# A three-stage FFT, routed-expert and dense kernel: the second stage's weights loaded by SyncE in halves, and its first layer's outputs taken in blocks of 128

## The chip, the cores and the metric

The kernel runs on one core of one Trainium2 chip. The metric is the device time of one execution in microseconds (us). Engines are named as in the profile: PE is TensorE (PEld its weight loads), ACT is ScalarE, DVE is VectorE, POOL is GpSimd, SP is SyncE. SP computes nothing here; it only issues DMA transfers. POOL issues the indirect ones (gathers and scatters by a list of row numbers).

## What is computed

```python
X = np.fft.fft(np.fft.fft(x, axis=1), axis=2)           # x: 8 x 3072 x 256
x = X.real.reshape(24576, 256)
logits = x @ w_gate                                     # 8 experts
e_idx = np.argmax(logits, axis=1)
gate_w = softmax(logits)[e_idx]; eom = sigmoid(x @ w_output_gate)
for e in range(8):                                      # each token to one expert
    m = e_idx == e
    out[m] = gate_w[m] * eom[m, e] * (np.maximum(x[m] @ w1[e], 0) @ w2[e])   # 256 -> 1024 -> 256
h = out @ w_in                                          # 256 -> 2048
return (h * sigmoid(1.702 * h)) @ w_out                 # 2048 -> 256
```

## The kernel before

Every factor of a matmul is held as a high and a low part (`h` and `l`, together nearly fp32), and a product is three matmuls: high by low, high by high, low by high. To split a tensor, ACT copies it into the high part (rounding it) and DVE subtracts that from the source to give the low part.

**Stage 1** (`phase1`, to about 309 us) makes the FFT of eight batches in 32 steps (`t` in the loop of L704), writes the result's rows to the DRAM tensor `xs` (SP, L515), and routes: DVE finds each token's expert and its place (`route`, L520), and POOL scatters row numbers and gate factors into per-expert lists in DRAM (`lst`, L612). Once the first four batches are routed, `cut` (L625) decides which tiles of 256 tokens can already be formed: for 40 tiles (`KA`) the expert (`owners`, L145) and the rows of the lists. `plan` (L778) does the same for the rest during stage 2.

**Stage 2** (`phase2`, L953) runs over 100 tiles of 256 tokens (`NALL`), sorted by expert, so that several tiles in a row belong to one expert. For a tile, POOL gathers the token rows from `xs` (L978, `xr`, two DMAs), PE transposes them (L1011, `xt`), ACT and DVE split them (L1014, L1015). A tile then has four turns `j`. In a turn, `hid` (L1034) makes 256 of the 1024 hidden values (24 matmuls, L1040 to L1042), ACT takes the high part with the ReLU (L1045, `hh`), DVE the low part (L1046, `hl`); `outp` (L1049) adds them to the tile's output (24 matmuls, L1059 to L1061) two turns later. After a tile's last `outp`, ACT scales the output by the gate (L1066, `yr`, two instructions) and POOL scatters the rows to the DRAM tensor `y` (L1068).

The weights of a tile's expert are loaded into one raw buffer per layer (`raw1`, `raw2`, 1 MB each) and split into one of two sets of high and low parts (`wps`, by the tile's parity). While tile `i` runs, `loop` (L1088) splits the weights of tile `i + 1` and asks for those of tile `i + 2`: turns 0 and 1 split `raw1` (two splits a turn, L1031 on ACT and L1032 on DVE), turns 2 and 3 split `raw2`. The loads are POOL gathers of one row per partition, issued at the end of turn 1 (`raw1`) and of turn 3 (`raw2`); a gather overwrites what the splits have just read. The row numbers (`widx`) come from `owners`: where a tile has the same expert as the one before it, 4096 is added, which is out of bounds, and the gather moves nothing.

```python
r1 = raw1.rearrange("p a (q c) -> p a c q", c=NFC)          # L1018
c = slice(2 * j, 2 * j + 2)
h, l, r = ws[i][0][:, :, c], ws[i][1][:, :, c], r1[:, :, c]  # first layer, L1028
h, l, r = ws[i][2][:, c], ws[i][3][:, c], raw2[:, c]         # second layer, L1030
```

Hidden block `c` of the first layer holds the outputs `8 q + c`, so a split of `raw1` reads every eighth element; a split of `raw2` reads unbroken runs. Partition `p` of `raw2` holds the rows `8 p` to `8 p + 7` of `w2`.

Between its own work stage 2 carries two other programs, a piece at a time: `conv.run` (L865) turns the dense layer's weights into stage 3's factors (DVE and some ACT, five pieces a tile; its loads `cv_raw`, 256 KB each, and its stores `scr` are SP's), and `rest` (L1151) issues the list scatters that stage 1 left over, `plan`, and the second list gather.

The program order on every engine is written by hand. `phase2` is a generator that `phase1` resumes: at step `NG - 2` (stage 1's buffers on the right side are given up; the raw buffers are made, SP reads tile 0's expert from `one` into a register and loads `raw1` and `raw2`, POOL gathers the lists, `lt`), at step `NG` (the lists are transposed into `xidx` and `scl`, the first token rows are gathered, tile 0's first layer is split), after the last step (tile 0's transposes and first `hid`), and then at every fourth of the remaining routing steps (L763 to L768), where after each step the rank matmuls that are due are issued (`flush`).

**Stage 3** (`phase3`, L1187) reads `y` and computes the dense layers in a seven-product scheme, PE without a break.

Of the kernel before, what the change touches and what calls it, by code (L numbers as in the profile page):

```python
# [18 lines left out]
P = 128  # L19
# [125 lines left out]
def owners(V, cum, ex, tmp, mi, widx, misc):  # L145

    n = mi.shape[1]
    ea = ex[:, 1 : 1 + n]
    for e in range(E):
        V.scalar_tensor_tensor(ea, mi, cum[:, e : e + 1], ea, ALU.is_ge, ALU.add)  # L150
# [4 lines left out]
    yield 0.3  # L155
    V.scalar_tensor_tensor(widx, ea, float(P), tmp, ALU.mult, ALU.add)
    yield 0.2


def phase1(tc, ctx, I, C, xs, lst, spd, kept, idn, then):  # L160
# [23 lines left out]
    ent, pis, keep, seen, widx, li, one = (kept[k] for k in ("ent", "pi", "keep", "seen", "widx", "li", "one"))  # L184
# [101 lines left out]
    el = cp.tile([P, 2, 3, 2, 8], F32R, name="el", tag="el")  # L286
# [338 lines left out]
    def cut():  # L625
# [14 lines left out]
        tmp = cp.tile([P, 96], F32, name="cut1", tag="el")[:, 0:KA]  # L640
        ni, ones, st, lr, ex = t[:, 0:8].bitcast(I32), t[:, 8:16], t[:, 16:24], t[:, 24:25], t[:, 32 : 33 + KA]
# [8 lines left out]
        V.memset(ex, 0.0)  # L650
        V.memset(ex[:, 0:1], -1.0)
        yield 0.3
        yield from tiles(cum, nt, st, ex, tmp, misc[:, 64 : 64 + KA], widx[:, 0:KA], misc)
        V.tensor_copy(one, ex[:, 1:2])
# [4 lines left out]
        yield 0.3  # L659

    def tiles(cum, nt, st, ex, tmp, mi, widx, misc):
        yield from owners(V, cum, ex, tmp, mi, widx, misc)

        V.tensor_scalar(st, nt, -1.0, float(LR), ALU.mult, ALU.add)
        V.scalar_tensor_tensor(st, cum, misc[:, 40:41], st, ALU.is_le, ALU.mult)
        yield 0.3
# [37 lines left out]
    for t in range(NG + 1):  # L704
        b, g = divmod(t, 4)
        if t == NG - 2:
            assert state["sc"] >= 24 * BC
# [33 lines left out]
        if t:  # L741
# [14 lines left out]
            if t == 4 * BC:  # L756
                queues["route"].append((cut(), BC - 1))
        if t < NG:
            if t:
                dims.append((Z, b, g))  # L760
    then.send((turns, scatter))
    n = 0
    while queues["route"]:  # L763
        step("route")
        flush(True)
        n += 1
        if n % 4 == 0 and n <= 12:
            then.send((None, None))  # L768
    for _ in range(max(0, 3 - n // 4)):
        then.send((None, None))  # L770
# [7 lines left out]
def plan(tc, C, kept, tot, pp):  # L778
# [3 lines left out]
    keep, seen, widx, li = (kept[k] for k in ("keep", "seen", "widx", "li"))  # L782
# [22 lines left out]
    ex = pp.tile([P, 1 + NTM - KA], F32, name="ex")  # L805
    V.memset(ex, 0.0)
    V.memset(ex[:, 0:1], -1.0)
    yield
    yield from owners(V, cum, ex, pp.tile([P, NTM - KA], F32, name="tmp"), mi, widx[:, KA:], misc)
# [143 lines left out]
def phase2(tc, ctx, I, xs, y, lst, scr, kept, C, idn, idf):  # L953
# [8 lines left out]
    hp = pool("p2h", 4, side="right")  # L962
    wps = [pool("p2w0", 1, side="right")]
    xp = pool("p2x", 2, side="right")
    rw = pool("p2r", 1, side="right")
    widx, li, one = (kept[k] for k in ("widx", "li", "one"))
    w1v = I["moe_w1"].rearrange("e (p a) f -> (e p) (a f)", a=2)
    w2v = I["moe_w2"].rearrange("e (p a) d -> (e p) (a d)", a=8)
    xidx = rw.tile([P, 2, 2, P], I32, name="xidx")
    scl = rw.tile([P, 2, P], F32, name="scl")  # L970
    lt = rw.tile([P, 2, P, 3], F32, name="lt")
    raw1 = rw.tile([P, 2, F1], F32, name="raw1")
    raw2 = rw.tile([P, 8, D], F32, name="raw2")
# [19 lines left out]
    def gather_w(i, k):  # L993
        if i < st["end"]:
            raw, src = ((raw1, w1v), (raw2, w2v))[k]
# [493 lines left out]
```

## Time and profile before

| | |
|---|---|
| median of 3 runs | 3627.42 us (3624.44 to 3629.73) |
| the profiled execution | 3622.02 us; its span 3620.1 us |
| mean granted PE clock | 0.987 |
| PE busy | 3492.8 us (96%) |
| DVE busy | 2478.4 us (68%) |
| ACT busy | 2557.9 us (71%) |
| POOL busy | 1186.0 us (33%) |
| DMA packets | 217.06 MB, mean 60 GB/s |

Busy times are of the whole span; a busy PE is not PE at its peak, since matmuls overlap. In rows that group instructions, the columns are: line, engine, operation, output <- inputs, shapes, count | busy time in us, mean ns of one | idle time of the engine just before them in us, and what ended most of it. "SPq" and the like stand for an engine's queue, which waits and issues.

### The profile page before, as it was taken

The numbers are of one execution on the slowest core, as the hardware profiler recorded it, in microseconds if no ns is written. First come the engines' busy times: TensorE is split into PE (matmuls) and PEld (weight loads), VectorE is DVE, ScalarE is ACT, GpSimd is POOL, SyncE is SP. The second block draws the span as 40 slices with busy tenths as digits, with TensorE's granted clock in tenths as the row PEclk, the third lists the DMA queues.
The fourth block names the chain that finished last, engine by engine and source line by source line (L and its number), as shares of the span: only waits on it lengthen the run. The fifth ranks groups of instructions, "written<-read, shape, count | busy, mean of one in ns | idle before, by whom it ended". The sixth has DMA issues, their size and how long they took to land.

```text
span 3620.1 us, 54703 instructions
## 1 busy us (share of the span) xinstructions
PE 3492.8 (96%) x20688; PEld 3118.2 (86%) x20688; DVE 2478.4 (68%) x3977; ACT 2557.9 (71%) x4457; POOL 1186.0 (33%) x988
## 2 busy tenths in 40 slices
PE   6998998999999999979999999999999999999999
PEld 5998898999999999978888888888888888888887
DVE  7886888888999899855555555555555555555554
ACT  5676777777888788856666666666666666666665
POOL 2774777866666666620000000000000000000000
PEclk9999999999999999989999999999999999999999
DMA  9763222222222222220000000000000000000000
GB/s 244 197 172 107 71 86 80 68 78 98 78 71 93 81 92 72 67 93 24 24 24 35 24 24 24 24 24 24 28 31 24 24 33 26 24 24 24 24 12 24
DMA packets 112899, 217.06 MB, mean 60 GB/s; under 512 B 42389, under 2 KB 77590, under 8 KB 102392
## 3 DMA queue, kind: packets, MB, share of 16 engines
q1 hardware_dynamic: 51352, 123.29, 11.0%
q0 software_dynamic: 60976, 89.98, 8.0%
q8 instruction: 163, 2.67, 0.3%
q14 instruction: 104, 0.85, 0.1%
q10 hardware_dynamic: 304, 0.26, 0.0%
HBM read 306.73 MB, written 83.86 MB: 108 GB/s over the span
## 4 chain that ended last, share of the span: by engine, by line
PE 70%; DVE 10%; ACT 8%; DMA 6%; issue 4%; POOL 1%; ACTq 0%; POOLq 0%; DVEq 0%; SPq 0%
PE acc L1370 10%; PE acc L1372 10%; PE acc L1371 10%; PE R L1305 5%; PE R L1307 5%; PE R L1306 5%; DMA raw<-in_moe_w,widx 4%; ACT w1h L1031 4%; DVE w1l L1032 3%; PE Q L1307 2%; PE Q L1305 2%; PE Q L1306 2%; PE yp L1061 2%; PE h L1040 2%; PE yp L1060 2%
## 5 line engine op out<-in xcount | busy, mean ns | idle before, releaser
L1227 DVE TENSOR_TENSOR g<-c,g 128x512 fp32r<-128x512 f32 x768 | 540.7, 706 | 136.9 <-ACT g L1212 128.6
L1370 PE MATMUL acc<-g,W 128*128 128x512 f32 x1536 | 605.7, 394 | 0.0
L1372 PE MATMUL acc<-g,W 128*128 128x512 f32 x1536 | 599.0, 390 | 0.0
L1371 PE MATMUL acc<-g,W 128*128 128x512 f32 x1536 | 598.1, 389 | 0.0
L1310 ACT ACTIVATE c<-c 128x512 f32<-128x512 f32 x576 | 364.7, 633 | 301.7 <-DVE c L1233 301.7
L1031 ACT CAST w1h<-raw 128x512 fp32r<-128x512 f32 x400 | 470.8, 1235 | 140.8 <-DMA raw<-in_moe_w,widx 140.8
L1032 DVE TENSOR_TENSOR w1l<-raw,w1h 128x512 fp32r<-128x512 f32 x400 | 460.2, 1185 | 122.7 <-ACT w1h L1031 121.8
L1230 POOL TENSOR_TENSOR xs<-xf,xf 128x512 f32<-128x512 f32 x46 | 69.9, 1519 | 1375.1 <-ACT g L1212 1375.1
L1212 ACT CAST g<-c 128x512 fp32r<-128x512 f32 x768 | 477.1, 621 | 24.4
L1061 PE MATMUL yp<-w2h,hl 128*128 128x256 f32 x1600 | 461.4, 288 | 30.0 <-DVE hl L1046 29.4
L1059 PE MATMUL yp<-w2l,hh 128*128 128x256 f32 x1600 | 455.7, 285 | 20.8 <-ACT hh L1045 20.7
L1040 PE MATMUL h<-xl,w1h 128*128 128x256 f32 x1600 | 462.1, 289 | 3.3 <-DVE xl L1015 3.3
L1042 PE MATMUL h<-xh,w1l 128*128 128x256 f32 x1600 | 455.4, 285 | 0.0
L1041 PE MATMUL h<-xh,w1h 128*128 128x256 f32 x1600 | 455.3, 285 | 0.0
L1060 PE MATMUL yp<-w2h,hh 128*128 128x256 f32 x1600 | 453.8, 284 | 0.0
L1233 DVE TENSOR_TENSOR c<-Q,u 128x512 f32<-128x512 f32 x192 | 132.8, 692 | 390.1 <-PE Q L1307 390.1
L1212 ACT COPY u<-R 128x512 f32<-128x512 f32 x192 | 112.7, 587 | 326.8 <-PE R L1307 326.8
L1061 PEld LDWEIGHTS yp<-w2h,hl 128*128 128x128 f32 x1600 | 306.7, 192 | 41.9 <-DVE hl L1046 41.4
L1372 PEld LDWEIGHTS acc<-g,W 128*128 128x128 f32 x1536 | 288.3, 188 | 61.2
L1371 PEld LDWEIGHTS acc<-g,W 128*128 128x128 f32 x1536 | 288.6, 188 | 57.4
L1370 PEld LDWEIGHTS acc<-g,W 128*128 128x128 f32 x1536 | 288.3, 188 | 56.9
L1059 PEld LDWEIGHTS yp<-w2l,hh 128*128 128x128 f32 x1600 | 306.9, 192 | 23.2 <-ACT hh L1045 23.2
(297 smaller groups left out, 8630.7 us busy)
## 6 DMA issues: line engine op xcount, KB each, us to landing
xs<-row SPq DMA_DIRECT2D x32, 768.0 KB, 5.5
out<-o SPq DMA_DIRECT2D x24, 1024.0 KB, 3.9
R<-in_xl SPq DMA_DIRECT2D x23, 1024.0 KB, 9.2
r<-y SPq DMA_DIRECT2D x23, 1024.0 KB, 4.7
cv_raw<-in_moe_w_in SPq DMA_DIRECT2D x16, 256.0 KB, 2.9
cv_raw<-in_moe_w_out SPq DMA_DIRECT2D x16, 256.0 KB, 3.7
xr<-xs,xidx POOLq DMA_INDIRECT x200
y<-yr,xidx POOLq DMA_INDIRECT x200
```

The source lines that it names most:

```text
L1031: A.copy(h, r)
L1032: V.tensor_tensor(l, r, h.bitcast(F32), ALU.subtract)
L1040: T.matmul(ps[:, a], w1h[:, dh, fc], xl[:, dh], start=(a == 0 and dh == 0), stop=False, skip_group_check=True)
L1042: T.matmul(ps[:, a], w1l[:, dh, fc], xh[:, dh], start=False, stop=(dh == 1), skip_group_check=True)
L1059: T.matmul(ps[:, s], hh[:, a, c], w2l[:, fc], start=(fc == 0 and s == 0), stop=False, skip_group_check=True)
L1060: T.matmul(ps[:, s], hh[:, a, c], w2h[:, fc], start=False, stop=False, skip_group_check=True)
L1061: T.matmul(ps[:, s], hl[:, a, c], w2h[:, fc], start=False, stop=(fc == NFC - 1), skip_group_check=True)
L1212: fn(*a)
L1227: V.tensor_tensor(l, src, h.bitcast(F32), ALU.subtract)
L1370: T.matmul(z, wh, gl, start=f, stop=False, skip_group_check=True)
L1371: T.matmul(z, wh, gh, start=False, stop=False, skip_group_check=True)
L1372: T.matmul(z, wl, gh, start=False, stop=la, skip_group_check=True)
```

## The change

Weights are no longer gathered by POOL. For each tile, SP reads the tile's expert from a list (`own`, made by `owners` in place of `widx`) into a register and loads each raw buffer in two halves of 512 KB from an address computed with it, one half per turn: the half whose two splits were issued in that turn. Every tile loads, whether or not the expert changed.

Hidden block `c` of the first layer now holds the outputs `128 c` to `128 c + 127`. A split of `raw1` takes four blocks of one half (`a`), 512 unbroken elements; before, two blocks of both halves. The second layer's rows follow: partition `p` of `raw2` holds row `128 a + p` in its block `a`, so that a half is loaded in runs of 1 KB, where the gather had 8 KB for each partition. The halves of `raw1` are runs of 4 KB.

`lt`, `xidx` and `scl` move into buffers that live through the kernel, and the scratch space for POOL's DMA descriptors is set to 8192.

The steps at which `phase1` resumes `phase2` move ahead: the list gather to step `NG - 5`, the lists' transposes to `NG - 3`, the four first loads and token gathers to `NG - 2`, two of tile 0's first-layer splits to `NG - 1` and two to `NG`. In the routing that is left after the last step, `phase2` is resumed at every third step up to the ninth, and the due rank matmuls are issued only after that.

```diff
-def owners(V, cum, ex, tmp, mi, widx, misc):
+def owners(V, cum, ex, mi, own):
+    V.memset(ex, 0.0)
     for e in range(E):
...
-    V.tensor_tensor(tmp, ea, ex[:, 0:n], ALU.is_equal)
-    V.tensor_scalar(tmp, tmp, 4096.0, misc[:, 40:41], ALU.mult, ALU.add)
-    V.scalar_tensor_tensor(widx, ea, float(P), tmp, ALU.mult, ALU.add)
+    V.tensor_scalar(own, ex, float(E - 1), None, ALU.min)
...
+        if t == NG - 5:
+            assert state["sc"] >= 24 * BC
+            then.send((None, None))
+        if t == NG - 3:
+            then.send((turns, None))
         if t == NG - 2:
             soon.close()
             then.send((None, None))
         if t == NG:
             zsoon.close()
-            then.send((turns, None))
+            then.send((None, None))
...
+        if t == NG - 1:
+            then.send((None, None))
...
         step("route")
-        flush(True)
         n += 1
-        if n % 4 == 0 and n <= 12:
-            then.send((None, None))
+        if n <= 9:
+            if n % 3 == 0:
+                then.send((None, None))
+        else:
+            flush(True)
...
-    w2v = I["moe_w2"].rearrange("e (p a) d -> (e p) (a d)", a=8)
+    w2v = I["moe_w2"].rearrange("e f d -> (e f) d")
...
-    def gather_w(i, k):
-        if i < st["end"]:
-            raw, src = ((raw1, w1v), (raw2, w2v))[k]
-            gather(raw.rearrange("p a f -> p (a f)"), src, widx[:, i : i + 1], E * P - 1)
+    def load_w(i, q):
+        if i >= st["end"]:
+            return
+        if q == 0:
+            st["e"] = nc.values_load(own[0:1, i : i + 1], engines=[mybir.EngineType.SP], min_val=0, max_val=E - 1)
+        if q < 2:
+            nc.sync.dma_start(raw1[:, q], w1v[bass.ds(st["e"] * P, P), q * F1 : (q + 1) * F1])
+        else:
+            h = NFC // 2 * (q - 2)
+            r = w2v[bass.ds(st["e"] * F1 + h * P, F1 // 2)]
+            nc.sync.dma_start(raw2[:, h : h + NFC // 2], r.rearrange("(a p) d -> p a d", p=P))
...
-            h, l, r = ws[i][0][:, :, c], ws[i][1][:, :, c], r1[:, :, c]
+            a, c = j // 2, slice(4 * (j % 2), 4 * (j % 2) + 4)
+            h, l, r = ws[i][0][:, a, c], ws[i][1][:, a, c], raw1[:, a].rearrange("p (c q) -> p c q", c=NFC)[:, c]
...
-                if j % 2:
-                    gather_w(i + 2, k)
-                elif extra is not None:
+                load_w(i + 2, j)
+                if j % 2 == 0 and extra is not None:
                     next(extra, None)
...
     turns, _ = yield
     lists(slice(0, KA), *turns(2))
+    yield
...
+    for q in range(4):
+        load_w(0, q)
     gather_x(0)
     gather_x(1)
-    for j in range(4):
+    yield
+    for j in range(2):
         split(0, 0, j)
-    gather_w(1, 0)
+    yield
+    for j in range(2, 4):
+        split(0, 0, j)
     turns, scatter = yield
     turn(0, turns(1)[0].bitcast(F32R).rearrange("p (a t) -> p a t", a=2))
+    load_w(1, 0)
+    load_w(1, 1)
...
-    nc = bacc.Bacc("TRN2", target_bir_lowering=False, num_devices=1)
+    nc = bacc.Bacc("TRN2", target_bir_lowering=False, num_devices=1, dynamic_dma_scratch_size=8192)
```

## Rows read from the trace of the kernel before

**Rows 1.** Busy time by stretch: us, busy us (instructions) per engine, PE clock, DMA share, GB/s.
```profile
309.00:345.00 36.00, 22.78 (x154) 21.96 (x153) 24.69 (x59) 22.54 (x45) 13.39 (x11) 0.76 0.25 76
...
760.00:1490.00 730.00, 714.07 (x5979) 707.83 (x5979) 667.84 (x1023) 603.65 (x917) 485.64 (x379) 1.00 0.25 82
1490.00:1580.00 90.00, 90.00 (x766) 90.00 (x765) 77.13 (x101) 74.64 (x114) 50.73 (x41) 1.00 0.13 41
1640.00:3600.00 1960.00, 1960.00 (x8844) 1621.02 (x8843) 1092.34 (x1618) 1315.36 (x2281) 126.99 (x91) 1.00 0.07 25
```
The engines stand in the order PE, PEld, DVE, ACT, POOL.

**Rows 2.** Timeline of ACT in stage 2: start us, us, what.
```profile
345.08 0.84 ACT L1066 ACTIVATE yr<-yp,scl 128x256 f32<-128x256 f32 x2
...
370.03 0.87 ACT L1066 ACTIVATE yr<-yp,scl 128x256 f32<-128x256 f32 x2
...
386.94 0.82 ACT L1066 ACTIVATE yr<-yp,scl 128x256 f32<-128x256 f32 x2
...
1498.94 0.85 ACT L1066 ACTIVATE yr<-yp,scl 128x256 f32<-128x256 f32 x2
...
1569.62 0.86 ACT L1066 ACTIVATE yr<-yp,scl 128x256 f32<-128x256 f32 x2
...
1589.23 0.84 ACT L1066 ACTIVATE yr<-yp,scl 128x256 f32<-128x256 f32 x2 [3.60 <-PE yp L1061]
```

**Rows 3.** Waits from 345 to 1590 us: us in total, times, longest.
```profile
ACT w1h L1031 <- DMA raw<-in_moe_w,widx: 139.9, 55, 8.6
...
PE yp L1061 <- DVE hl L1046: 29.4, 47, 1.5
```

**Rows 4.** The chain that ended last, 364 to 385 us: start us, us, what.
```profile
378.11 6.30 DMA raw<-in_moe_w,widx
```

**Rows 5.** DMA from 345 to 1590 us; last line: from 289.3 to 300.4 us.
```profile
DMA packets 54059, 96.31 MB, mean 77 GB/s; under 512 B 33115, under 2 KB 33116, under 8 KB 50096
...
q0 software_dynamic: 48752, 82.48, 20.2%
...
DMA packets 1708, 3.38 MB, mean 304 GB/s; under 512 B 212, under 2 KB 1452, under 8 KB 1452
```

**Rows 6.** Groups of instructions by line and shape, whole run.
```profile
L1031 ACT CAST w1h<-raw 128x512 fp32r<-128x512 f32 x400 | 470.8, 1235 | 140.8 <-DMA raw<-in_moe_w,widx 140.8
...
L1032 DVE TENSOR_TENSOR w1l<-raw,w1h 128x512 fp32r<-128x512 f32 x400 | 460.2, 1185 | 122.7 <-ACT w1h L1031 121.8
...
L1032 DVE TENSOR_TENSOR w2l<-raw,w2h 128x512 fp32r<-128x512 f32 x400 | 261.3, 697 | 0.0
L978 POOL DMA_INDIRECT raw<-in_moe_w,widx x198 | 237.2, 1198 | 218.4 <-DVE w2l L1032 99.3 <-DVE fi L555 17.0 <-DVE w1l L1032 16.0
L1031 ACT CAST w2h<-raw 128x512 fp32r<-128x512 f32 x400 | 232.3, 647 | 0.0
```

**Rows 7.** SP's instructions of L1120 and L1122: duration ns min/median/max.
```profile
L1120 SPq TENSOR_LOAD <-one x1: 484/484/484, 288.2 to 288.2; - x1
...
L1122 SPq DMA_DIRECT2D raw<-in_moe_w x1: 600/600/600, 289.9 to 289.9; - x1
```

**Rows 8.** Landings: SP's two raw loads, two cv_raw loads (321 us), issues (median us last).
```profile
DMA to landing us min/median/max: 7.0/8.7/10.5
...
L875 SPq DMA_DIRECT2D cv_raw<-in_moe_w_in x2: 327/376/424, 320.8 to 321.2; - x2
...
DMA to landing us min/median/max: 2.7/2.8/3.0
...
xs<-row SPq DMA_DIRECT2D x32, 768.0 KB, 5.5
...
scr<-cv_w SPq DMA_DIRECT2D x3, 512.0 KB, 2.8
```

**Rows 9.** Timelines of PE and (last line) ACT, 306 to 333 us; in brackets idle before.
```profile
314.30 0.75 PE L1011 MATMUL d<-idn,xr 128*128 128x128 f32 x4 [5.14 <-ACT L L486]
...
307.08 4.38 ACT L1031 CAST w1h<-raw 128x512 fp32r<-128x512 f32 x4
```

More of the change, by code (lines that the diff above doesn't have):

```diff
@@ L183, in phase1 @@
     t3 = p23.tile([P, 3, 2, 2, NW3], F32R, name="t3")
-    ent, pis, keep, seen, widx, li, one = (kept[k] for k in ("ent", "pi", "keep", "seen", "widx", "li", "one"))
+    ent, pis, keep, seen, own, li = (kept[k] for k in ("ent", "pi", "keep", "seen", "own", "li"))
     td = cp.tile([P, 4, 290], F32R, name="td")
@@ L285, in phase1 @@
     eh = cp.tile([P, 2, 3, 2, 8], F32R, name="eh", tag="eh")
-    el = cp.tile([P, 2, 3, 2, 8], F32R, name="el", tag="el")
+    el = cp.tile([P, 2, 3, 2, 8], F32R, name="el")
     blank = cp.tile([P, 48, 3], F32, name="blank")
@@ L639, in cut @@
         t = cp.tile([P, 96], F32, name="cut0", tag="eh")
-        tmp = cp.tile([P, 96], F32, name="cut1", tag="el")[:, 0:KA]
-        ni, ones, st, lr, ex = t[:, 0:8].bitcast(I32), t[:, 8:16], t[:, 16:24], t[:, 24:25], t[:, 32 : 33 + KA]
+        ni, ones, st, lr, ex = t[:, 0:8].bitcast(I32), t[:, 8:16], t[:, 16:24], t[:, 24:25], t[:, 32 : 32 + KA]
         nt, cum = seen[:, 0], seen[:, 1]
@@ L649, in cut @@
         V.tensor_tensor_scan(cum, ones, nt, 0.0, ALU.mult, ALU.add)
-        V.memset(ex, 0.0)
-        V.memset(ex[:, 0:1], -1.0)
+        yield 0.2
+        yield from owners(V, cum, ex, misc[:, 64 : 64 + KA], own[:, 0:KA])
+        V.tensor_scalar(st, nt, -1.0, float(LR), ALU.mult, ALU.add)
+        V.scalar_tensor_tensor(st, cum, misc[:, 40:41], st, ALU.is_le, ALU.mult)
         yield 0.3
-        yield from tiles(cum, nt, st, ex, tmp, misc[:, 64 : 64 + KA], widx[:, 0:KA], misc)
-        V.tensor_copy(one, ex[:, 1:2])
         V.tensor_reduce(lr, st, AX.X, ALU.add)
@@ L764, in phase1 @@
         step("route")
-        flush(True)
         n += 1
-        if n % 4 == 0 and n <= 12:
-            then.send((None, None))
-    for _ in range(max(0, 3 - n // 4)):
+        if n <= 9:
[3 more added lines that the diff above has]
+            flush(True)
+    for _ in range(max(0, 3 - n // 3)):
         then.send((None, None))
@@ L781, in plan @@
     V = nc.vector
-    keep, seen, widx, li = (kept[k] for k in ("keep", "seen", "widx", "li"))
+    keep, seen, own, li = (kept[k] for k in ("keep", "seen", "own", "li"))
     misc = pp.tile([P, 64], F32, name="misc2")
@@ L804, in plan @@
     yield
[L805 to L809, printed above, removed]
+    ex = pp.tile([P, NTM - KA], F32, name="ex")
+    yield from owners(V, cum, ex, mi, own[:, KA:])
     V.tensor_scalar(st, nb, -1.0, float(LR), ALU.mult, ALU.add)
@@ L961, in phase2 @@
     pool = lambda name, bufs, c=ctx, **k: c.enter_context(tc.tile_pool(name=name, bufs=bufs, reuse_waits="tile", **k))
[L962 to L966, printed above, removed]
-    w1v = I["moe_w1"].rearrange("e (p a) f -> (e p) (a f)", a=2)
-    w2v = I["moe_w2"].rearrange("e (p a) d -> (e p) (a d)", a=8)
[L969 to L973, printed above, removed]
+    own, li, lt, xidx, scl = (kept[k] for k in ("own", "li", "lt", "xidx", "scl"))
+    w1v = I["moe_w1"].rearrange("e (p a) f -> (e p) (a f)", a=2)
+    w2v = I["moe_w2"].rearrange("e f d -> (e f) d")
     NFC = F1 // P
@@ L1172, in phase2 @@
             st["end"] = NTM
-            for k in range(2):
-                gather_w(NALL, k)
+            for q in range(4):
+                load_w(NALL, q)
             for j in range(4):
@@ L1179, in phase2 @@
             gather_x(NALL + 1)
-            gather_w(NALL + 1, 0)
+            for q in range(2):
+                load_w(NALL + 1, q)
             for j in range(4):
                 split(NALL, 1, j)
-            gather_w(NALL + 1, 1)
+            for q in range(2, 4):
+                load_w(NALL + 1, q)
             loop(NALL, NTM, [], iter(()))
@@ L1430, in program @@
             "seen": kp.tile([P, 2, E], F32, name="seen"),
-            "widx": kp.tile([P, NTM], I32, name="widx"),
+            "own": kp.tile([P, NTM], I32, name="own"),
             "li": kp.tile([P, 1], I32, name="li"),
-            "one": kp.tile([P, 1], I32, name="one"),
+            "lt": kp.tile([P, 2, P, 3], F32, name="lt"),
+            "xidx": kp.tile([P, 2, 2, P], I32, name="xidx"),
+            "scl": kp.tile([P, 2, P], F32, name="scl"),
             "ent": kp.tile([P, NSLOT, 3], F32, name="ent"),
```

26 lines of the change are left out of this document (10 added, 16 removed).

## Prediction

> **What bounds the kernel now.** I read the busy time by stretch first [rows 1]. From 1640 us on, the third stage keeps TensorE busy without a break, and the change doesn't touch it. What can move lies before: the end of the first stage (309 to 345 us, TensorE busy 22.8 of 36 us and granted 0.76 of its clock, so at 1.2 instead of 2.4 GHz for part of it) and the second stage's 100 tiles.
>
> Next, the pace of a tile. The first yr of a tile starts at 345.08 us for tile 0 and at 1589.23 us for tile 99 [rows 2], so 99 intervals take 1244.2 us: 12.57 us each. Near the end, where the weight conversion is done and the expert no longer changes, six intervals take 1569.62 - 1498.94 = 70.7 us: 11.78 us each. Is that TensorE's own floor? From 1490 to 1580 us it is busy in all of the 90 us, at the full clock [rows 1]. So 11.78 is the floor for the same matmuls, and the stage lies 99 x (12.57 - 11.78) = 78 us above it.
>
> Where are those 78 us? The waits of the stage [rows 3] show ACT standing 139.9 us, in 55 places, in front of a w1h split until a weight gather has landed, and TensorE itself waiting 29.4 us for hl, which comes late behind it. The chain shows such a gather at 378 us with 6.30 us [rows 4]; the tile around it lasts from 370.03 to 386.94, 16.9 us [rows 2]. It is a change of expert, and only these move data: POOL's queue has 82.5 MB in this stretch [rows 5], of which the x and y rows of some 98 tiles are 0.52 MB a tile, 51 MB; the remaining 31.5 MB are weights for 15 tiles of 2.1 MB. The other gathers find their index out of bounds.
>
> **The splits.** A w1 split takes 1235 ns on ACT and 1185 ns on DVE; a w2 split of the same 128x512 elements, read in unbroken runs, 647 and 697 ns [rows 6]. With the new split w1 reads unbroken runs too, so I take the w2 prices: 400 x 588 ns = 235 us off ACT and 400 x 488 ns = 195 us off DVE, 2.35 and 1.95 us a tile. DVE is busy 667.8 of 730 us in the middle of the stage, 11.5 of 12.57 us a tile, and ACT 10.4 [rows 1]; they go to about 9.5 and 8.0. None of it counts directly, for TensorE's 11.78 us cover both. It removes what makes hl and hh late when a tile begins with two w1 splits in each of its first two turns.
>
> **The loads.** Removed are 198 gathers on POOL of 1198 ns, with 218 us of POOL's idle time in front of them, in which the x gathers and y scatters behind them stood [rows 6]. Added on SP are, for each tile, one register load (0.48 us) and four issues; the longer of the two such issues that exist took 0.60 us [rows 7]. Ahead of the first stage's last xs stores SP gets four such issues where it had two, 1.2 us more, and those stores have buffers of their own. That is 2.9 us of SP a tile, where it mostly waits. Each issue waits until DVE has split the half it overwrites. Queued behind it on SP stand the conversion's cv_raw loads, for which DVE waits; they are asked for one converted block ahead (over ten steps at five a tile, two tiles), so a delay of a few us costs nothing.
>
> Today a w1 gather leaves only when two of a tile's four turns are over. In the new order a half is asked for as soon as its two splits are done and is needed one tile later: 11.8 us less about 2.0 us for the splits and 1.2 us to issue leaves 8.6 us for landing. Bounds for a half of 512 KB: 2.7 us (256 KB of cv_raw) and 10.5 us (the second of two 1 MB loads while the queues are full) [rows 8]. Nearest are a 512 KB store in rows of 4 KB, 2.8 us, for the w1 halves, and the 768 KB xs stores in 1 KB runs, 5.5 us, for the w2 halves [rows 8]. I take 3 to 5.5 us, inside the 8.6; so the 139.9 us of ACT's waits go, the changes of expert included.
>
> The cover has a price: each tile now moves its 2.1 MB, also where the expert stays. At 77 GB/s over 12.57 us a tile moves 0.97 MB today, 0.32 of it weights; then it is 0.97 - 0.32 + 2.10 = 2.75 MB in 11.85 us, 232 GB/s. In a stretch where the queues were full they moved 304 GB/s [rows 5], so 76% of them are in use. Prefetched x and buffered y stand a tile off and shouldn't notice. If they do, or if TensorE's pace suffers from this traffic, a tile is longer. I take 0.07 us for it and for the conversion's vector work between the splits: **11.85 us a tile, -71 us** (bounds: 11.78, -78; 12.57, 0).
>
> A rule speaks against the halves. The two cv_raw loads that SP issued at 320.8 and 321.2 us both landed within 3.0 us of their issue [rows 8], so transfers issued together overlap. The Trainium skill ("DMA: Bandwidth & Descriptors", Rules for kernel authors) wants 1 MiB or more per DMA and, in its anatomy of a DMA from GpSimd, counts 2.0 us plus bytes/436e3. An estimate by that page is 3.2 us for a half; four paid one after the other would make 12.8 us a tile and 99 x 0.23 = 23 us more instead of 71 less.
>
> **The end of the first stage.** The second stage's list gather, its transposes, the first weight loads and half of tile 0's splits move ahead, between matmuls that run anyway. TensorE idles there 5.14 us behind ACT [rows 9], and some more behind xl and DVE's routing. Ahead of the row copies that end the 5.14 us, ACT has four w1h splits, 4.38 us [rows 9]; two faster ones, 1.2 us, stay there: 3.2 us. DVE saves as much, but its routing chain still decides the rest. Bounds: nothing (the moved splits push the same copies before), and 13 us (all that TensorE isn't busy from 309 to 345 us [rows 1]). I take **-5 us**; the rank matmuls that are no longer flushed at once give the last two of it. Index arithmetic, the smaller DMA scratch and the moved tiles cost nothing I can price: the new owner list has a few vector operations fewer, and POOL now issues less into that scratch.
>
> **Sum.** The profiled execution took 3622.0 us for its 3620.1 us span: 3622.0 - 71 - 5 = 3546. The median of the runs is 3627.4, 5.4 above it: **3551 us**.
>
> **Rivals.**
> - *Part of the gain* (0.15). Some halves or y scatters are late at 76% use of the queues; a tile is 12.3 us: -27 - 4, 3596. For it: with full queues one load did take 10.5 us [rows 8], over the 8.6.
> - *The new split isn't faster* (0.06): ACT and DVE keep their loads, the waits for gathers go all the same, and with DVE at 11.5 us a tile under a floor of 11.78 some of hl's lateness stays; I give it 12.1 us a tile, a third of the way back, 3627 - 46 = 3581. Against it: the w2 rows.
> - *Each tile becomes a change of expert* (0.05): the load stands on ACT's path in every tile, at the price of the 16.9 us tile: 99 x (16.91 - 12.57) = 430 us, 4057. It decides once a half lands later than 8.6 us after its issue. For it: the traffic is unconditional. Against it: those gathers left half a tile later, in one piece.
> - *The halves go one after the other* (0.03): each waits on its queue for the one before it, 2 x 2.8 + 2 x 5.5 = 16.6 us a tile from the rows, +399, 4026. The overlapping cv_raw loads speak against it. (By the page of the Trainium skill named above it would be 3650.)
> - *No change* (0.03): DVE or POOL hold the tile at 12.5 us by their order alone, 3622.
>
> **Numbers.** The forecast's own case has 0.68. It, the first rival and the second are faster by over 0.2% (7 us, about what a measurement of this kernel can tell): 0.89; same 0.03; the two loaded rivals are slower: 0.08. The forecast's own range is 3536 (floor tile, all 13 us) to 3571 (12.0 us a tile, no gain before it). With the first two rivals taken in, and 5 us below for the spread of the runs, it is 3530 to 3600, which leaves out some 0.15.
>
> **What would show it.** Right: w1 splits near 650 and 700 ns; no wait of ACT for raw; yr intervals of 11.8 to 11.9 us from the first tiles on; POOL without raw; SP's loads landing in 3 to 6 us; traffic of some 230 GB/s. Wrong: ACT still idle until raw lands, with intervals over 12.2 us; tiles over 11.8 us with TensorE busy throughout; or a first stage that ends later than before.

## The result, and the profile after

The changed kernel takes 3547.38 us (median of 4 runs, 3544.93 to 3549.83), the kernel before 3626.49 us beside it: a ratio of 0.9781 with a 95% interval of [0.9764, 0.9798], 79 us less. The profiled execution took 3546.35 us, its span 3544.4 us. The forecast was 3551 us, 3546 for the profiled execution.

First the stretches, as in [rows 1]: us, then busy us (instructions) of PE, PEld, DVE, ACT and POOL, the clock, the DMA share and GB/s.

```profile
309.00:345.00 36.00, 24.64 (x180) 23.96 (x181) 22.86 (x63) 21.38 (x52) 6.32 (x6) 0.81 0.62 194
345.00:760.00 415.00, 415.00 (x3497) 415.00 (x3496) 338.82 (x643) 275.17 (x538) 244.01 (x212) 1.00 0.83 232
760.00:1490.00 730.00, 730.00 (x6148) 730.00 (x6147) 570.75 (x1020) 482.36 (x940) 312.61 (x265) 1.00 0.73 233
```

From 345 to 1490 us TensorE is busy without a break. In the middle DVE fell from 667.8 to 570.8 us and ACT from 603.7 to 482.4, and the traffic rose from 82 to 233 GB/s. Where the time came from, the timeline of ACT tells, with the first yr of tile 0 and of tile 99 [rows 2]:

```profile
340.39 0.84 ACT L1058 ACTIVATE yr<-yp,scl 128x256 f32<-128x256 f32 x2 [0.81 <-PE yp L1053]
...
1513.48 0.84 ACT L1058 ACTIVATE yr<-yp,scl 128x256 f32<-128x256 f32 x2 [3.72 <-PE yp L1053]
```

The 99 intervals take 1173.1 us where they took 1244.2: 11.85 us a tile instead of 12.57, **-71.1 us**. Tile 0 comes 4.7 us earlier; the runs below show that this is not the change's doing. From the last yr to the end of the span it is 2031.0 us, and 2030.8 before: the third stage is unchanged.

The splits by line and shape, beside [rows 6]:

```profile
L1024 DVE TENSOR_TENSOR w2l<-raw,w2h 128x512 fp32r<-128x512 f32 x400 | 259.9, 690 | 0.0
L1024 DVE TENSOR_TENSOR w1l<-raw,w1h 128x512 fp32r<-128x512 f32 x400 | 258.1, 687 | 100.2 <-ACT w1h L1023 100.2
L1023 ACT CAST w1h<-raw 128x512 fp32r<-128x512 f32 x400 | 228.0, 624 | 0.0
L1023 ACT CAST w2h<-raw 128x512 fp32r<-128x512 f32 x400 | 227.6, 624 | 0.0
```

A w1 split now costs what a w2 split does, 624 and 687 ns instead of 1235 and 1185. The longest waits from 345 to 1510 us, where [rows 3] had ACT in front of raw with 139.9 us:

```profile
POOL y L1060 <- ACT yr L1058: 469.4, 95, 9.1
ACT hh L1037 <- PE h L1034: 202.8, 191, 2.3
ACT xh L1007 <- PE xt L1004: 108.4, 96, 1.1
DVE xl L1008 <- ACT xh L1007: 93.0, 92, 1.0
DVE w1l L1024 <- ACT w1h L1023: 92.9, 96, 1.4
```

No wait for raw is left, and none of TensorE's for hh or hl: the other engines wait for TensorE. SP's issues of the weights, with the landing of all 400 loads, and the traffic from 345 to 1510 us [rows 5, 7, 8]:

```profile
L985 SPq DMA_DIRECT2D raw<-in_moe_w x200: 332/346/930, 286.9 to 1484.1; - x100
...
L989 SPq DMA_DIRECT2D raw<-in_moe_w x200: 383/384/740, 288.3 to 1488.3; - x100
...
DMA to landing us min/median/max: 2.9/4.6/10.5
```

```profile
DMA packets 156301, 267.51 MB, mean 230 GB/s; under 512 B 15150, under 2 KB 114479, under 8 KB 156167
...
q1 hardware_dynamic: 135522, 215.24, 59.7%
q0 software_dynamic: 20645, 50.54, 15.4%
```

A half lands in 4.6 us on the median. POOL's queue went from 82.5 to 50.5 MB. At the end of the first stage, the timeline of ACT, with two rows that [rows 9] answer to:

```profile
303.75 1.05 ACT L482 ACTIVATE row<-d 128x256 f32<-128x256 f32 x2 [2.57 <-DMA xs<-row]
...
305.99 0.55 ACT L359 ACTIVATE Z<-zs 128x384 fp32r<-128x384 f32 x1
...
307.32 2.25 ACT L1023 CAST w1h<-raw 128x512 fp32r<-128x512 f32 x4
```

All four w1h splits of tile 0 still stand at their old place, in 2.25 us instead of 4.38. The wait of 2.57 us in the first row is new: the row buffers wait for the xs stores, which SP issues behind the four weight loads. It stands in every profile with the changed order that was taken on the first two chips (2.0 to 5.7 us), and in none with the old order; on the last two chips it is absent.

### The profile page after: what moved, and what is told of

It is laid out like the page before. It is cut to its first block, busy times and chain, and to the rows that moved or that the text cites. A ratio compares the mean times of both kernels' runs of the same rounds, so it can differ in the third digit from the quotient of the medians.

```text
span 3544.4 us, 56230 instructions
## 1 busy us (share of the span) xinstructions
PE 3472.7 (98%) x20688; PEld 3111.2 (88%) x20688; DVE 2296.4 (65%) x3970; ACT 2338.9 (66%) x4457; POOL 891.5 (25%) x790
## 4 chain that ended last, share of the span: by engine, by line
PE 92%; DVE 2%; DMA 2%; ACT 1%; issue 1%; POOL 0%; SPq 0%; DVEq 0%; ACTq 0%; POOLq 0%
PE acc L1375 10%; PE acc L1377 10%; PE acc L1376 10%; PE h L1032 5%; PE h L1033 5%; PE h L1034 5%; PE yp L1051 5%; PE yp L1053 5%; PE yp L1052 5%; PE R L1310 5%; PE R L1312 5%; PE R L1311 5%; PE Q L1312 2%; PE Q L1310 2%; PE Q L1311 2%; PE S L1311 1%
## 5 line engine op out<-in xcount | busy, mean ns | idle before, releaser
L1053 PE MATMUL yp<-w2h,hl 128*128 128x256 f32 x1600 | 453.9, 284 | 0.0
L1060 POOL DMA_INDIRECT y<-yr,xidx x200 | 246.3, 1231 | 548.8 <-ACT yr L1058 500.1
L1037 ACT ACTIVATE hh<-h 128x512 fp32r<-128x512 f32 x400 | 240.1, 600 | 208.7 <-PE h L1034 208.7
L1024 DVE TENSOR_TENSOR w1l<-raw,w1h 128x512 fp32r<-128x512 f32 x400 | 258.1, 687 | 100.2 <-ACT w1h L1023 100.2
L1038 DVE SCALAR_TENSOR_TENSOR hl<-h,hh 128x512 fp32r<-128x512 f32 x400 | 274.0, 685 | 60.3 <-ACT hh L1037 58.4
```

What stands on the lines that cost most here:

```text
L1053: T.matmul(ps[:, s], hl[:, a, c], w2h[:, fc], start=False, stop=(fc == NFC - 1), skip_group_check=True)
```

## The experiments

The theory at first: the loads carry the gain, because halves asked for early take ACT's wait for raw away; the shorter splits only help. The rival: the splits carry it. Below, a tile's length is the distance of the first yr of tile 0 to that of tile 99, by 99. Runs of the first four kernels come from one chip, of the next four from a second, of the next three from a third and of the last from a fourth; each ratio is to the kernel before on the same chip.

### The old split in the changed kernel

```diff
-    w2v = I["moe_w2"].rearrange("e f d -> (e f) d")
+    w2v = I["moe_w2"].rearrange("e (p a) d -> (e p) a d", a=8)
...
-            nc.sync.dma_start(raw2[:, h : h + NFC // 2], r.rearrange("(a p) d -> p a d", p=P))
+            nc.sync.dma_start(raw2[:, h : h + NFC // 2], w2v[bass.ds(st["e"] * P, P), h : h + NFC // 2])
...
-raw1[:, a].rearrange("p (c q) -> p c q", c=NFC)[:, c]
+raw1[:, a].rearrange("p (q c) -> p c q", c=NFC)[:, c]
```

> The changed kernel with the first layer's blocks taken every eighth element again (and w2's rows to match, loaded in runs of 4 KB); SP still loads halves, one a turn. Theory L, the loads made the gain: w1 splits go back to about 1235 and 1185 ns, but no gather is waited for, so a tile stays near TensorE's floor, 11.9 to 12.0 us, and the run near 3550 to 3560 us. Theory S, the splits made it: DVE at 11.3 us a tile and ACT at 10 leave hl and hh late as before; 12.3 us a tile or more, 3590 us and up.

It took 3556.47 us, ratio 0.9828 [0.9806, 0.985]. The splits are long again, in the groups by shape:

```profile
L1022 ACT CAST w1h<-raw 128x512 fp32r<-128x512 f32 x400 | 452.8, 1192 | 0.0
L1023 DVE TENSOR_TENSOR w1l<-raw,w1h 128x512 fp32r<-128x512 f32 x400 | 445.4, 1146 | 65.0 <-ACT w1h L1022 63.8
```

But a tile takes 11.87 us, and TensorE is busy in all of the 730 us from 760 to 1490. So the loads alone bring the tile to its floor.

```profile
760.00:1490.00 730.00, 730.00 (x6147) 730.00 (x6146) 675.37 (x1027) 607.54 (x943) 353.49 (x268) 1.00 0.72 233
```

### The new split in the kernel before

This kernel pairs hidden values with other rows of w2, so that its time is read and not its output.

```diff
-            h, l, r = ws[i][0][:, :, c], ws[i][1][:, :, c], r1[:, :, c]
+            a, c = j // 2, slice(4 * (j % 2), 4 * (j % 2) + 4)
+            h, l, r = ws[i][0][:, a, c], ws[i][1][:, a, c], raw1[:, a].rearrange("p (c q) -> p c q", c=NFC)[:, c]
```

> The kernel before with only the first layer's split read in unbroken runs; the gathers stay with POOL. It pairs hidden values with other rows of w2, so its output is another one; the work is the same. Theory L: the tiles that change the expert keep 15 to 16 us and ACT's waits for raw stay above 100 us; 12.3 us a tile or more, 3595 us and up. Theory S: waits for raw shrink to the changes of expert alone and the other tiles go to 11.9; 15 x 4 us are left, 12.3 at most, near 3590 us or below. If both parts are needed, e1 and this one each keep a part of the 79 us.

It took 3542.37 us, ratio 0.979 [0.9773, 0.9807]: as large a gain as that of the whole change, from an edit of two lines, without one of SP's loads in stage 2 and with the program order as before. A tile takes 11.82 us. The waits from 345 to 1510 us and the middle of the stage:

```profile
ACT w1h L1032 <- DMA raw<-in_moe_w,widx: 52.7, 31, 5.2
```

```profile
760.00:1490.00 730.00, 730.00 (x6196) 730.00 (x6195) 576.82 (x1028) 488.08 (x950) 439.00 (x391) 1.00 0.25 82
```

ACT still waits 52.7 us for gathers, and TensorE mostly doesn't notice: with short splits what comes late is made up before TensorE needs it. Only five intervals, at changes of expert in the first 30 tiles, are over 13 us. Because of them the first 30 intervals take 362.2 us in sum, and 356.4 in the changed kernel. The other 69 take 807.5 against 816.7, since this kernel's matmuls follow each other faster (118.9 against 119.9 ns; the section on small tiles finds why). That is worth 96 x 1 ns x 99, some 9 us, and isn't the splits' doing: at the changed kernel's pace this run would have saved about 65 of the 71 us. So either part alone gives nearly all of the gain, and both theories fall as I had put them.

### Whole loads instead of halves

```diff
-        if q < 2:
-            nc.sync.dma_start(raw1[:, q], w1v[bass.ds(st["e"] * P, P), q * F1 : (q + 1) * F1])
-        else:
...
+        if q == 1:
+            nc.sync.dma_start(raw1.rearrange("p a f -> p (a f)"), w1v[bass.ds(st["e"] * P, P)])
+        elif q == 3:
+            nc.sync.dma_start(raw2, w2v[bass.ds(st["e"] * F1, F1)].rearrange("(a p) d -> p a d", p=P))
```

> The changed kernel with two loads of 1 MB a tile in place of four of 512 KB, asked for after turn 1 and after turn 3, where the gathers stood. Theory, earliness is what hides them: a half is needed 8.6 us after it is asked for, the whole of raw1 only some 5 us after, and 1 MB lands in 6 to 9 us at this traffic; ACT waits 1 to 4 us in each tile, 13 to 15 us a tile, 3660 to 3860 us, slower than before. Rival, SP in place of POOL is enough: 11.9 us a tile, 3547 us.

3548.07 us, ratio 0.9807 [0.9786, 0.9828], 11.85 us a tile. A wait comes back and costs nothing, as the list of waits and the row of the middle show:

```profile
ACT w2h L1021 <- DMA raw<-in_moe_w: 82.3, 53, 4.0
```

```profile
760.00:1490.00 730.00, 730.00 (x6147) 730.00 (x6146) 570.89 (x1020) 485.49 (x944) 312.10 (x266) 1.00 0.71 232
```

The halves, and that the first of each pair is asked for one turn earlier, are not what the gain hangs on. The rule that the prediction weighed (the Trainium skill, "DMA: Bandwidth & Descriptors", Rules for kernel authors: 1 MiB or more per DMA) is not borne out as a cost here: four halves a tile and two whole loads give 11.85 us both. TensorE covers the loads in both, so what halves would cost where nothing covers them is not shown.

### Weights loaded for two tiles only

The output is another, since all later tiles use the weights of the first two loads.

```diff
-        if i >= st["end"]:
+        if i >= st["end"] or i >= 2:
```

> The changed kernel that loads weights for tiles 0 and 1 only; all later tiles split what stands in the raw buffers, so all tokens get those weights. It leaves out 98 of 100 loads and SP's register loads. In the changed kernel a tile takes 11.88 us where the quiet end of the kernel before had 11.78, and matmuls start 119.9 ns apart where they had 118.9. Theory T, the traffic costs TensorE that 1 ns: back to 11.78 us a tile, 10 us less, 3537 us. Rival, the full queue of TensorE has this pace by itself: 11.88 us and 3547 us without the traffic too.

3550.8 us, ratio 0.9815 [0.9794, 0.9835]; 11.85 us a tile, at 56 GB/s instead of 233 (the row is 760 to 1490 us):

```profile
760.00:1490.00 730.00, 730.00 (x6148) 730.00 (x6147) 571.03 (x1022) 484.63 (x945) 314.02 (x266) 1.00 0.18 56
```

TensorE does 6148 instructions there with and without the traffic. What the changed kernel keeps above the 11.78 us of [rows 2] isn't the price of the loads.

### Twice the traffic

```diff
+    junk = nc.dram_tensor("junk", [16, P, F1], F32, kind="Internal").ap()
...
+        if i >= 2:
+            nc.sync.dma_start(junk[(4 * i + q) % 16], w1v[0:P, 0:F1])
```

> The changed kernel, and from tile 2 on SP issues one more DMA behind each half, 512 KB from the weights to a scrap of DRAM, so that a tile asks for about 4.85 MB instead of 2.75. Nothing reads the scrap. The queues moved 304 GB/s in the stretch of the kernel before where they were full; at that rate 4.85 MB take 16 us. Theory cover (the loads cost nothing as long as a half lands within 8.6 us of its issue, and everything beyond that stands on ACT's path): halves land later than 8.6 us, ACT waits for raw in most tiles, and a tile takes the 16 us that its bytes need, 3547 + 98 x 4.1 = 3950. Rival (the queues have more room than those 304 GB/s, or copies from DRAM to DRAM share them otherwise): at over 410 GB/s a tile stays at 11.85 us, 3550. Rival (a transfer costs by its issue on SP, 0.4 us each, not by its bytes): 3550 too, but with halves that land as in the changed kernel, 4.6 us.

3811.5 us, ratio 1.0512 [1.0485, 1.054], 14.48 us a tile. Three of its waits (345 to 1600 us), and its traffic from 345 to 1500 us:

```profile
ACT w2h L1026 <- DMA raw<-in_moe_w: 364.1, 166, 5.2
...
ACT w1h L1026 <- DMA raw<-in_moe_w: 194.3, 147, 5.3
...
PE yp L1056 <- DVE hl L1041: 89.9, 156, 6.8
```

```profile
DMA packets 171934, 380.79 MB, mean 330 GB/s; under 512 B 17572, under 2 KB 97445, under 8 KB 171824
...
raw<-in_moe_w SPq DMA_DIRECT2D x312, 512.0 KB, 12.2
```

The cover ends as the theory says: halves land after 12.2 us, over the 8.6, ACT and then TensorE wait, and a tile lasts as long as its bytes take, 4.78 MB at 330 GB/s. The queues gave 330 and not 304 GB/s, hence 3812 and not 3950. So the changed kernel, at 233 GB/s, has about 100 to spare.

### Every tile gathers, in the kernel before

```diff
-    V.tensor_scalar(tmp, tmp, 4096.0, misc[:, 40:41], ALU.mult, ALU.add)
+    V.tensor_scalar(tmp, tmp, 0.0, misc[:, 40:41], ALU.mult, ALU.add)
```

> The kernel before, with the out-of-bounds index taken away: every tile gathers its weights through POOL, 1 MB a layer, asked for after turns 1 and 3. It prices the third rival of the prediction, each tile a change of expert, in the kernel whose splits still read every eighth element. Theory (a late gather and the slow splits make a tile longer together): each tile takes about what a change of expert takes in the kernel before, 15 to 17 us, so 3627 + 84 x 2.5 to 4.5 us, 3840 to 4000. Rival (what made a tile of the kernel before long was the slow splits alone, and its changes of expert add little): intervals of 12.5 to 13 us, 3620 to 3670.

3715.45 us, ratio 1.0247 [1.0219, 1.0276]; 13.50 us a tile, between the two expectations. Its waits from 345 to 1600 us:

```profile
ACT w1h L1031 <- DMA raw<-in_moe_w,widx: 275.2, 92, 9.8
DVE w1l L1032 <- ACT w1h L1031: 207.3, 165, 8.9
```

ACT waits for the gather in nearly every tile, 3 us each. A change of expert thus costs about 1 to 2 us a tile when it is the rule, not the 4.3 us of the single 16.9 us tile of [rows 2].

### The drain of the routing as before

```diff
         step("route")
+        flush(True)
         n += 1
-        if n <= 9:
-            if n % 3 == 0:
-                then.send((None, None))
-        else:
-            flush(True)
+        if n % 4 == 0 and n <= 12:
+            then.send((None, None))
```

> The changed kernel with the routing after the last step as before: the due rank matmuls are issued after every step, and the second stage is resumed at every fourth of them. The prediction gave this part about 2 of the 5 us that the first stage's end gained. Theory: the first yr of tile 0 starts 1 to 3 us later than the 340.39 us of the changed kernel, the tiles are the same, 3548 to 3551. Rival (the moved steps before the drain and the short splits make all of the 5 us): 340.4 within 0.5 us, 3547. Rival (the drain makes most of it): 344 us or later.

3551.39 us, ratio 0.9797 [0.9775, 0.9818]. Tile 0's yr starts at 346.19 us, and the third expectation seems to hold. But the last copy of Z (the FFT's end) stands later too, on ACT's timeline:

```profile
310.32 0.55 ACT L359 ACTIVATE Z<-zs 128x384 fp32r<-128x384 f32 x1
...
346.19 0.84 ACT L1056 ACTIVATE yr<-yp,scl 128x256 f32<-128x256 f32 x2 [0.81 <-PE yp L1051]
```

From that copy to the first yr it is 35.9 us here; in the changed kernel 340.39 - 305.99 = 34.4; in the kernel before 39.5 (from 305.59 to the 345.08 of [rows 2]). I had read the start of tile 0 from the span's start, which mixes in when the FFT ended. It isn't the chip that makes this copy late: in the run with a gather in every tile, on the same chip with the old order, it stands at 305.74 us. The repeat below comes back to this.

### Small tiles that move the operands

The two traces left one thing that I couldn't explain: in the changed kernel matmuls of stage 2 start 119.9 ns apart, in the kernel before 118.9, at the same granted clock of 1.00. That the traffic does it had fallen. (A tile has 96 of these matmuls: 12 in each `hid` and 12 in each `outp`, not 24.) In the kernel before, the second of the two that stream w2's high part starts 117.2 ns behind the first in odd tiles and 119.8 in even ones. The compiled program puts the even tiles' weights at the upper end of SBUF, the on-chip memory that the engines read (its right side), and the odd ones' on the left. Divided by 256, the byte addresses of all operands on the right leave 224 in both kernels; those of the left set leave 0 before (it starts at 77568) and 224 after (75488). Below, two operands are alike when they leave the same. Each of these runs adds unused tiles:

```diff
+    pool("p2a", 1, side="right").tile([P, 8], F32, name="pad")
     hp = pool("p2h", 4, side="right")
...
                 wp = ctx.enter_context(tc.tile_pool(name="w2", bufs=1, reuse_waits="tile"))
+                wp.tile([P, 8], F32, name="pad")
```

> The changed kernel with two tiles of 32 bytes a partition, one at the start of the second stage's buffers on the right side of SBUF and one ahead of those on the left, so that all operands of the matmuls of stages 2 and 3 start at a multiple of 64 bytes; in the changed kernel they all start 32 bytes past one. In the kernel before the odd tiles' weights started at a multiple of 64 and the rest did not. There the matmuls that stream the odd tiles' w2 high part followed each other at 117.1 ns and those of the even tiles at 119.8; in the changed kernel both take 120.0. Theory placement: with all operands moved, the matmuls of stage 2 follow each other at 116 to 117 ns, a tile takes 11.5 us or so, 99 x 0.3 = 30 us less, and stage 3, whose operands move too, may gain as well: 3515 or less. Rival (the placement does nothing, and the 1 ns comes from POOL's fewer DMAs or from SP's loads): 119.9 ns, 11.85 us, 3547. Rival (only w2, as the streamed operand, matters, and in half of the matmuls): 118.5 ns, 3535.

3532.26 us, ratio 0.9737 [0.9716, 0.9758], 11.69 us a tile: half of what the theory asked. The odd tiles' matmuls follow each other at 116.8 ns, the even ones' stay at 119.9. The next two change the 8 of the tile on the right to 56 and to 24.

> As the run with two small tiles, but the one on the right takes 224 bytes a partition instead of 32, so that the operands on the right side of SBUF (x, hh, hl and the even tiles' weights) start at a multiple of 256 bytes like the odd tiles' weights on the left; with 32 bytes they started 192 bytes past one. There the second layer's matmuls of odd tiles followed each other at 116.4 to 117.3 ns and those of even tiles stayed at 119.7 to 120.0. Theory placement at a multiple of 256: the even tiles take 117 too, hence 118.3 to 116.8 ns on the mean, 96 matmuls by 1.5 ns = 0.15 us a tile, 11.55 us, and 15 us less than that run: 3517; less again if x and hh count by themselves. Rival (the side or the height in SBUF decides, or the buffers' distance): even tiles stay at 120, 11.69 us, 3532.

> The same with 96 bytes a partition on the right, so that the operands there start at a multiple of 128 bytes that is none of 256. If 128 decides: even tiles at 117 ns, 11.55 us a tile, as with 224 bytes. If 256 decides: even tiles at 120 ns and 11.69 us, as with 32 bytes. If neither decides, 11.69 us here and with 224 bytes.

11.85 and 11.77 us a tile; 3570.44 us, ratio 0.9813 [0.9773, 0.9854], and 3553.1 us, ratio 0.9772 [0.9722, 0.9823], in profiles where tile 0 starts 32 and 15 us later than in the changed kernel's, so that the pace is what counts. Both of my theories fell: with everything at a multiple of 256 each tile was slow, odd and even.

> The changed kernel once more, for the end of the first stage. In four profiles whose first stage has the same instructions as the changed kernel's, up to the loads behind it, tile 0's first yr started at 340.4, 342.9, 346.2 and 346.6 us, in two with the kernel before's first stage at 345.1 and 348.3. If the -5 us of the prediction is real, this one starts near 340.4; if it is the spread of the routing's end, it falls anywhere from 340 to 347, with tiles of 11.85 us and 3545 to 3552 either way.

3569.72 us, ratio 0.9824 [0.9784, 0.9863], 65 us less than the kernel before beside it, with the same 11.85 us a tile. Tile 0 starts at 354.16 us: neither expectation. The last copy of Z stands at 318.46, and from there it is 35.7 us. By this measure nine profiles with the changed order and the short splits give 34.4 to 36.4 us (the one with twice the traffic 35.0); the two with the order and the splits of before give 39.5 and 42.5; the kernel before with the new split alone gives 34.7, the changed kernel with the old split 37.2, the old drain 35.9. So behind the FFT some 3 to 8 us are gained, the new split alone gives that, and the drain gives nothing that can be seen.

But the last copy of Z is itself moved by the change. The twelfth copy from the end comes where the moved steps begin (272.60 us in the changed kernel, 1.8 us behind the moved list gather). From it to the last copy it is 27.7 to 27.8 us in the three profiles with the old order, and 30.8 to 41.7 in all eleven with the changed one. The stretch in the kernel before, in the changed kernel and in the kernel before with the new split, and what TensorE waits for there in the changed kernel:

```profile
277.77:305.59 27.82, 27.20 (x173) 26.17 (x172) 9.69 (x49) 17.73 (x62) 11.17 (x13) 1.00 0.66 181
```

```profile
272.60:305.99 33.39, 29.92 (x182) 28.94 (x181) 9.94 (x50) 18.40 (x63) 22.20 (x24) 0.95 0.64 173
```

```profile
278.73:306.56 27.83, 27.04 (x172) 26.02 (x172) 9.68 (x49) 17.75 (x61) 11.18 (x14) 1.00 0.68 181
```

```profile
274.80 1.00 PE L1074 MATMUL d<-idf,lt 128*128 128x128 f32 x4 [2.10 <-DMA lt<-lst,li]
```

The transposes of the lists now stand ahead of the FFT's last matmuls and wait for the list gather; the row copies wait for the xs stores; and the granted clock is below 1.00 in ten of the eleven. From the twelfth copy to tile 0's first yr it is 67.8 us in the changed kernel and 67.3 in the kernel before (62.5 with the new split alone, 65.8 to 77.7 in the other ten with the changed order). So the short splits gain about 5 us at the end of the first stage, and in the changed kernel the moved steps lose them again; which of their parts costs how much, no run separates. (The four longest, 74.5 and more, come from the last two chips, where the old order was not profiled.) The 4.7 us by which tile 0 came earlier arose before the moved steps: the twelfth copy stands at 272.60 instead of 277.77 us, and anywhere from 271.9 to 295.0 in the eleven profiles with this first stage.

The last run takes the difference between a matmul's two operands as what counts. It keeps the first padding and adds:

```diff
     hp = pool("p2h", 4, side="right")
+    pool("p2b", 1, side="right").tile([P, 48], F32, name="pad")
     wps = [pool("p2w0", 1, side="right")]
+    pool("p2c", 1, side="right").tile([P, 16], F32, name="pad")
     xp = pool("p2x", 2, side="right")
...
     xp = ctx.enter_context(tc.tile_pool(name="p3x", bufs=1))
+    xp.tile([P, 16], F32, name="pad")
```

> The changed kernel with small tiles that move buffers in SBUF and do nothing else: in stage 2 both sets of weights start at a multiple of 256 bytes, and x, hh and hl 192 bytes past one; in stage 3 the weights at a multiple of 256 and the data 64 bytes past one. So far, where a tile's weights and its data started at the same place modulo 256 bytes (all tiles of the changed kernel, 32 bytes past a multiple of 64 each, and all of the run with everything at a multiple of 256), matmuls followed each other at 120.0 ns; where they differed (the odd tiles of the kernel before by 32 bytes, of the first padded run by 64, of the second by 128), those of the second layer took 117 to 119, 116 to 117 and 118 to 119 ns. Theory offset: what counts is the difference between the two operands of a matmul, so that now both parities take 116 to 117.5 ns, 96 by 3 ns or 0.3 us a tile, 11.53 to 11.6 us, and stage 2 ends 25 to 34 us earlier than in the changed kernel, 8 to 17 earlier than with the first padding: 3515 to 3525 against 3547. Stage 3 may gain by the same, up to 8860 by 3 ns, 27 us more. Rival (only the set of weights on the left side gains, by its place there): 11.69 us as with the first padding, 3532. Rival (it is the parity, chance or the chip): 11.85, 3547.

Stage 2 does what the theory says: 11.51 us a tile, 116.0 ns in even and odd tiles alike, 33.8 us less than the changed kernel's. The first yr of tile 0 and of tile 99:

```profile
357.32 0.84 ACT L1058 ACTIVATE yr<-yp,scl 128x256 f32<-128x256 f32 x2 [0.77 <-PE yp L1053]
...
1496.63 0.84 ACT L1058 ACTIVATE yr<-yp,scl 128x256 f32<-128x256 f32 x2 [3.48 <-PE yp L1053]
```

Stage 3 does the opposite: from tile 99's first yr to the end 2047.4 us instead of 2031.0, 16.4 us longer, its matmuls of 512 columns 229.0 ns apart instead of 227.1. In the same 1860 us the changed kernel does 8395 matmuls and this run 8324:

```profile
1640.00:3500.00 1860.00, 1860.00 (x8395) 1538.09 (x8394) 1036.80 (x1536) 1248.93 (x2167) 121.52 (x88) 1.00 0.07 25
```

```profile
1640.00:3500.00 1860.00, 1860.00 (x8324) 1526.31 (x8323) 1027.45 (x1524) 1239.08 (x2149) 119.04 (x85) 1.00 0.07 25
```

With tile 0 at 357.32 us (340.39 in the changed kernel), the run comes out at 3548.01 us, ratio 0.9766 [0.9742, 0.979], and not at the 3515 to 3525 of the theory.

The rows of 760 to 1490 us say it for stage 2 without any distance of starts, since TensorE is busy throughout and only the count of its instructions differs. Padded by 224 bytes (weights and data alike), by 96 (left set 128 off), by 32 (left set 64 off), and the last run (both sets 64 off):

```profile
760.00:1490.00 730.00, 730.00 (x6147) 730.00 (x6147) 574.14 (x1033) 482.49 (x940) 310.92 (x264) 1.00 0.74 233
```

```profile
760.00:1490.00 730.00, 730.00 (x6187) 730.00 (x6186) 575.34 (x1029) 486.06 (x947) 315.44 (x268) 1.00 0.75 234
```

```profile
760.00:1490.00 730.00, 730.00 (x6228) 730.00 (x6228) 577.32 (x1033) 489.98 (x955) 315.38 (x267) 1.00 0.74 234
```

```profile
760.00:1490.00 730.00, 730.00 (x6345) 730.00 (x6344) 583.98 (x1043) 497.34 (x969) 316.83 (x269) 1.00 0.75 236
```

The changed kernel has 6148, as many as the run with all alike within one. The version with the first padding beats both kernels: its interval lies below that of the changed kernel and below that of the old drain beside it on the same chip. The last run without its tile in stage 3 wasn't run; by the parts it should be near 3511, an estimate: the changed kernel's 3547 less 33.8 and the 2.6 us or so that stage 3 gained with the first padding.

## Why the prediction was right, and where its steps were not

**The bound.** Right. The stage stood 78 us above TensorE's floor, and 71.1 of them went, where 71 was forecast.

**The splits.** The prices were right (647 and 697 ns taken, 624 and 687 measured). "None of it counts directly" undersold them: the new split alone gives nearly all of the stage's gain. The prediction looked for one cause of the late hh and hl, the gathers that ACT waits for. There were two that had to meet, a late gather and two long splits behind it, and removing either is nearly enough. The sum was right because the gain is bounded by the floor, not because each part had its share.

**The loads.** 4.6 us to land lies in the 3 to 5.5 taken, 0.35 to 0.38 us an issue below the 0.60, and 230 GB/s is the 232 worked out. The run with twice the traffic, whose halves land after 12.2 us and are waited for, fits the 8.6 us of slack; at this traffic it wasn't needed: whole loads, the first half asked for one turn later, cost nothing either.

**The 0.07 us above the floor.** Right in size and wrong in its reason. It was put down to the traffic and to the conversion; without the traffic it stays. It is the pace of the matmuls, which the placement set. "The smaller DMA scratch and the moved tiles cost nothing I can price" is the step that failed here: the odd tiles' weights moved by 2080 bytes and lost their offset to the data, 119.9 instead of 118.9 ns, and 96 x 1 ns x 99, some 10 us, were lost by it.

**The end of the first stage.** This step failed, and that its number came out is luck. Tile 0's first yr came 4.7 us earlier where 5 were forecast, but this execution was ahead by 5.2 us before the moved steps began. From there on the change gained nothing: 67.8 us against 67.3. Two effects cancel. Behind the FFT 39.5 - 34.4 = 5.1 us are gained, by the splits: all four stay ahead of the row copies, not two, so they give 4.38 - 2.25 = 2.1 us and not 3.2; the rank matmuls give nothing that can be seen; what remains comes with the new split too, since that alone reaches 34.7, and DVE's shorter halves of the splits are the likely rest, but no run separates them. Ahead of the FFT's end the moved steps, "between matmuls that run anyway", cost 33.4 - 27.8 = 5.6 us, which the prediction had at nothing. "Those stores have buffers of their own" was wrong as well: the row copies waited 2.57 us for them.

**The rivals.** None of the prices was reached. That of splits that stay slow, 12.1 us a tile, is what the old split in the changed kernel measures: 11.87. That of a change of expert in each tile, 430 us, came from a single tile at the start of the stage and was far too high: with the slow splits and a gather in every tile it was 13.50 - 12.57 = 0.93 us a tile, 92 us. The halves did not go one after the other.

## What to carry to other kernels

Where an engine stands a known distance above its floor because others feed it late, look for all that has to meet to make them late: removing any one of it can give nearly the whole gain, and a second repair then adds little. Before a change that moves buffers is priced at zero, look at where they come to lie: compare the pace of the same matmuls by buffer. And measure the start of a stage from the last event that the change can't move, not from the start of the run and not from an event that the moved work itself delays, as the FFT's end did here.

## What the runs showed of the hardware

**The placement of a matmul's operands.** In stage 2, at a granted clock of 1.00, matmuls of 256 columns followed each other at 119.4 to 119.9 ns on the mean of a tile's when both operands were alike (the same place modulo 256 bytes; all tiles of the changed kernel and of five more runs 119.9, even tiles of the others 119.4 to 119.9). With the weights 32, 64 or 128 bytes off the data it was 118.1 to 118.3, 116.0 to 116.8 and 118.7 ns. Both being at a multiple of 256 does not help (119.9). A difference by 64 or by 128 was faster than none, so being alike modulo 64 or 128 isn't what makes it slow. Matmuls of 512 columns in stage 3 went the other way: 226.8 to 227.1 ns with both alike, 229.0 with the data 64 bytes off. Within the first of these, 226.8 (the padded runs) against 227.1 (the changed kernel and the kernel before) isn't explained by the place modulo 256, which is 0 in the padded runs and in the kernel before alike. Other differences weren't tried, and what lies behind all this is open.

**Every eighth element.** Reading 512 values of 4 bytes a partition in steps of 32 bytes cost ACT 1235 instead of 624 ns and DVE 1185 instead of 687, nearly twice.
